# Attention and two MLPs on one core: token blocks of the second MLP widened from 256 to 384

## The chip, the cores and the metric

The kernel runs as one program on one core of a Trainium2 chip. The metric is device time in microseconds (us) of one execution; a kernel's time is the median of its runs. A profiled execution gives besides its own time a span, from the first to the last instruction in the trace.

## What is computed

Everything is float32 outside the kernel. Attention (4 batches, 8 heads, 576 positions, head size 64, with a position bias) gives x with 2304 tokens of 512 values. Two MLPs follow, each fed by the one ahead of it:

```python
def _moe_ref(x, w_in, w_out):          # d_ff = 2048
    h = x @ w_in
    g = h - np.tanh(h)
    return g @ w_out

def _moe2_ref(x, w_gate, w_val, w_out):  # d_ff = 1536
    gate = 1.0 / (1.0 + np.exp(-(x @ w_gate)))
    val = x @ w_val
    return gate * val @ w_out
```

The change concerns the second MLP alone.

## The kernel before

TensorE multiplies in float32r, a form of lower precision, so each operand is split into a high and a low part and every product is made of three matmuls: high by high, low by high and high by low.

The program has three stages: the bias with the attention (the trace's first third), the first MLP, and the second MLP. Both MLPs are one list of steps, `STEPS` (L433 to L435). A step (kind, b, f) treats one block b of `TBS[kind]` tokens and one slice f of the hidden size. In the first MLP (kind 1) a block has 384 tokens and a step two slices of 128 hidden values. In the second (kind 2) a block has 256 tokens before the change, a step one slice of 128, and a block twelve steps (f = 0 to 11): 9 blocks, 108 steps, numbered 48 to 155.

A step of the second MLP passes through these stages, and the main loop of `mlps` puts the stages of several steps into each of its iterations:

- `first` (L589): gate and value projection. For each of the two, 4 parts of the inner size by 3 products, so 24 matmuls, weights stationary, tokens moving: as wide as the block. They write one of two PSUM buffers `up` (L709).
- `second` (L597): sigmoid of the gate on ScalarE (ACT), L611.
- `third` (L613): gate by value on VectorE (DVE), L632; it reads `up` last and so frees it for the `first` two steps on.
- `fourth` (L634): high part by a cast on ACT (L639), low part by a subtraction on GpSimd (POOL, L640).
- `fifth` (L648): output projection. Here the tokens are stationary, 128 at a time, and 512 columns of the weight move: 3 matmuls for each 128 tokens (L670), accumulated over the twelve steps of the block in one PSUM buffer `acc` for each 128 tokens. The pool has four (L720).
- `sixth` (L680): after a block's last step each accumulator is copied to a tile `o`, in turn by ACT (L694) and DVE (L692), and sent to `out` (L698). The pool of `o` has two buffers (L766).

`LAGS` (L771) gives the distances: in iteration n the loop issues `second` of step n-1, `third` of n-2, `fourth` of n-3, then `sixth` of a step that ended a block in the iteration before, `first` of n, and `fifth` of n-4. TensorE therefore does `first`(n), `fifth`(n-4), `first`(n+1), and so on, in that order.

Beside this a stream of weights is prepared: a weight tile is loaded (L484), its magnitude taken on ACT (`scan`, L493), four DVE operations build the float32 value (L508, L509, L510, L506), and ACT and POOL split it (L526, L524). `load` for the next tile is issued when the last DVE operation of one is done. `conv_rate` (L775) gives one or two such tiles for each step. The stream ends in the first block of the second MLP; after that its weights stay in SBUF.

Tokens for the next block are loaded by `x_load` (L564) and split by `x_split` (ACT L570, POOL L571) seven to two steps ahead.

Of the kernel before, what the change touches and what calls it, by code (L numbers as in the profile page):

```python
# [414 lines left out]
KIND = {0: "VV", 2: "V", 4: "VV", 6: "AG", 7: "AG", 8: "AG"}  # L415


TBS = (None, 384, 256)
NF1, NF2 = DF1 // 128, DF2 // 128
FA = 8  # L420
RES = 34
# [10 lines left out]
HALF = FA // NPR  # L432
STEPS = [(1, b, f) for b in range(NT // TBS[1]) for f in range(HALF)]  # L433
STEPS += [(1, b, f) for b in range(NT // TBS[1]) for f in range(HALF, NF1 // NPR)]
STEPS += [(2, b, f) for b in range(NT // TBS[2]) for f in range(NF2)]  # L435
LAST = {(k, f): n for n, (k, b, f) in enumerate(STEPS)}
# [112 lines left out]
def mlps(tc, st, xr, W, xs, x2s, out, consts):  # L549
# [9 lines left out]
    def x_load(blk, kt):  # L559
        kind, b, half = blk  # L560
        TB = TBS[kind]
        m = xr.tile([128, TB], F32, name="xm")
# [4 lines left out]
    def x_split(blk, kt):  # L567
        m = xraw.pop((blk, kt))
        t = xh.tile([128, 2, TBS[blk[0]]], F32R, name="xt")
        A.copy(t[:, 0], m)  # L570
# [9 lines left out]
    def project(w, blk, p):  # L580
        TB = TBS[blk[0]]
        for kt in range(4):
            x = xt[blk, kt]
            for i, (a, c) in enumerate(P3):
                T.matmul(p[:, 0:TB], w[:, a, 128 * kt:128 * kt + 128], x[:, c], start=(kt == 0 and i == 0), stop=(kt == 3 and i == 2))  # L585
# [299 lines left out]
```

## Time and profile before

| what | value |
|---|---|
| median of 3 runs | 1224.86 us (1223.2 to 1227.69) |
| the profiled execution | 1225.91 us |
| its span, first to last instruction | 1224.1 us |
| TensorE matmul busy | 1192.4 us (97%) |
| DVE, ACT, POOL busy | 731.8, 641.1, 570.5 us |
| chain that ended last | PE 88%, DVE 5%, DMA 3%, ACT 2% |
| second MLP in the span | from 745.1 us to the end |

Busy time of TensorE counts a matmul from its start to a modelled end, and neighbours overlap; the cost of a matmul in a stream is read from start to start. A timeline row merges like instructions that follow each other: "x24" has a start, and the time until the last of the 24 ended. "[0.79 <-DVE t L632]" at a row's end is idle time of the engine before it and what ended it.

### The profile page before, as it was taken

How to read it: one execution, taken by the hardware profiler on the slowest of the kernel's cores; microseconds unless marked ns; L12 is line 12 of the kernel's file. 1: busy time of each engine (PE TensorE's matmuls, PEld its weight loads, DVE VectorE, ACT ScalarE, POOL GpSimd, SP SyncE). 2: the span in 40 equal slices, each digit the busy share in tenths (PEclk: the TensorE clock that was granted, in tenths of full speed). 3: DMA queues.
4: the chain of work that ended last, by engine and by line, in shares of the span. 5: the costliest groups of instructions: out<-in, count | busy, mean ns of one | idle time of the engine just before them, and what ended most of it. 6: DMA issues, size and time to landing. Idle time of an engine off the chain costs nothing.

```text
span 1224.1 us, 21207 instructions
## 1 busy us (share of the span) xinstructions
PE 1192.4 (97%) x7856; PEld 1053.9 (86%) x7856; DVE 731.8 (60%) x1292; ACT 641.1 (52%) x1338; POOL 570.5 (47%) x584
## 2 busy tenths in 40 slices
PE   7889999999999999999999999999999999999998
PEld 2257777777679999999999999889999999999997
DVE  6888999999739888988989669851101111011010
ACT  5887888888657667667666564432112121121211
POOL 1049989998635555555645334552122121221211
PEclk9999999999989999999999999999999999999999
DMA  6765747475212333333343313420001000010000
GB/s 188 248 195 149 230 144 215 140 231 151 79 49 87 112 122 107 104 121 103 135 146 130 106 57 109 148 79 13 27 10 35 22 15 26 10 36 18 18 18 18
DMA packets 80631, 120.86 MB, mean 99 GB/s; under 512 B 10256, under 2 KB 55056, under 8 KB 80528
## 3 DMA queue, kind: packets, MB, share of 16 engines
q1 hardware_dynamic: 80528, 119.51, 31.4%
q8 instruction: 62, 1.02, 0.4%
q14 instruction: 41, 0.34, 0.1%
HBM read 89.71 MB, written 29.77 MB: 98 GB/s over the span
## 4 chain that ended last, share of the span: by engine, by line
PE 88%; DVE 5%; DMA 3%; ACT 2%; issue 1%; SPq 0%; POOL 0%; DVEq 0%; ACTq 0%; POOLq 0%
PE up L585 39%; PE acc L662 15%; PE acc L670 11%; PE sc L231 7%; PE pv L323 6%; PE pt L273 6%; PE bt L71 2%; PE pv L320 1%; DMA wraw<-in_wo 1%; DMA bsc<-e 1%; DVE y L66 1%; DVE wu L510 1%; DVE wu L506 1%; DMA wraw<-in_wv 1%; PE pf L277 1%
## 5 line engine op out<-in xcount | busy, mean ns | idle before, releaser
L585 PE MATMUL up<-xt,w 128*128 128x256 f32 (+1 forms) x3744 | 536.3, 299 | 4.7 <-DVE t L632 2.8
L585 PEld LDWEIGHTS up<-xt,w 128*128 128x128 f32 x3744 | 524.7, 190 | 16.3 <-DVE t L632 5.4
L640 POOL TENSOR_TENSOR gl<-t,gh 128x256 fp32r<-128x256 f32 (+1 forms) x204 | 184.7, 914 | 464.7 <-ACT gh L639 296.9
L632 DVE TENSOR_TENSOR t<-up,t 128x256 f32<-128x256 f32 x108 | 45.6, 423 | 319.4 <-ACT t L611 319.4
L611 ACT ACTIVATE t<-up 128x256 f32<-128x256 f32 x108 | 41.5, 384 | 328.0 <-PE up L585 327.8
L662 PE MATMUL acc<-gh,w 128*128 128x384 f32 x768 | 195.8, 335 | 2.9 <-ACT z L604 2.9
L662 PEld LDWEIGHTS acc<-gh,w 128*128 128x128 f32 x768 | 137.9, 188 | 4.8 <-ACT z L604 3.8
L670 PE MATMUL acc<-w,gh 128*128 128x512 f32 x432 | 135.6, 395 | 0.0
L263 POOL TENSOR_SCALAR n<-n,rec 128x576 f32<-128x576 f32 x144 | 117.6, 828 | 26.2 <-ACT n L253 18.4
L662 PE MATMUL acc<-gl,w 128*128 128x384 f32 x384 | 128.3, 334 | 0.0
L253 ACT ACTIVATE n<-n,mn 128x576 f32<-128x576 f32 x144 | 112.6, 782 | 22.9 <-DVE mn L246 21.7
L246 DVE CUSTOM_DVE_ANT_0 n<-sc,bias 128x576 f32<-128x576 f32 x144 | 107.3, 745 | 22.4 <-POOL n L263 13.5
L571 POOL TENSOR_TENSOR xt<-xm,xt 128x384 fp32r<-128x384 f32 (+1 forms) x84 | 75.3, 909 | 71.9 <-ACT xt L570 71.9
L524 POOL TENSOR_TENSOR w<-wu,w 128x512 fp32r<-128x512 f32 x68 | 99.5, 1464 | 12.4 <-ACT w L526 11.1
L639 ACT CAST gh<-t 128x256 fp32r<-128x256 f32 (+1 forms) x204 | 91.4, 453 | 7.5 <-PE acc L662 3.6
L273 PE MATMUL pt<-ident,n 128*128 128x128 f32 x576 | 90.9, 281 | 0.0
L273 PEld LDWEIGHTS pt<-ident,n 128*128 128x128 f32 x576 | 66.8, 142 | 27.6 <-POOL n L263 7.9
L625 ACT ACTIVATE z<-z,c 128x768 f32<-128x768 f32 x48 | 45.2, 942 | 77.7 <-DVE up L624 77.7
L231 PE MATMUL sc<-kh,qs 128*128 128x288 f32 x336 | 81.2, 327 | 3.5 <-DVE mn L246 3.2
L670 PE MATMUL acc<-w,gl 128*128 128x512 f32 x216 | 84.0, 389 | 0.0
L670 PEld LDWEIGHTS acc<-w,gh 128*128 128x128 f32 x432 | 74.5, 190 | 9.8
L626 DVE TENSOR_TENSOR t<-up,t 128x768 f32<-128x768 f32 x48 | 46.0, 958 | 60.9 <-ACT t L604 60.9
(70 smaller groups left out, 1699.3 us busy)
## 6 DMA issues: line engine op xcount, KB each, us to landing
wraw<-in_wo SPq DMA_DIRECT2D x28, 512.0 KB, 3.7
bsc<-e SPq DMA_DIRECT2D x36, 295.5 KB, 3.1
raw<-in_qT SPq DMA_DIRECT2D x64, 144.0 KB, 4.1
raw<-in_kT SPq DMA_DIRECT2D x64, 144.0 KB, 2.9
xm<-xs SPq DMA_DIRECT2D x48, 192.0 KB, 3.6
x2s<-o SPq DMA_DIRECT2D x48, 192.0 KB, 3.9
wraw<-in_wi SPq DMA_DIRECT2D x16, 512.0 KB, 4.4
wraw<-in_wg SPq DMA_DIRECT2D x12, 512.0 KB, 3.7
```

The source lines that it names most:

```text
L231: T.matmul(s[:, hf, x:x + n], w, k_[:, a, y:y + n], start=(i == 0), stop=(i == len(ops) - 1 and x + n == S // 2))
L246: V.tensor_tensor_reduce(n.rearrange("p (a b) -> p a b", a=2), s[:, :, 0:288], bias[t].rearrange("p (a b) -> p a b", a=2), -0.125, 3.0e38, ...
L253: A.activation(n, n, AF.Exp, bias=m, scale=-1.0, accum_out=nsum[u, t // 3][:, t % 3:t % 3 + 1])
L263: G.tensor_scalar(n, n, nrec[u, t // 3][:, t % 3:t % 3 + 1], 1.0, ALU.mult, ALU.mult)
L273: T.transpose(pt[:, i], n[:, o:o + 128], ident)
L524: self.nc.gpsimd.tensor_sub(w[:, 1], u, w[:, 0].bitcast(F32))
L571: G.tensor_sub(t[:, 1], m, t[:, 0].bitcast(F32))
L585: T.matmul(p[:, 0:TB], w[:, a, 128 * kt:128 * kt + 128], x[:, c], start=(kt == 0 and i == 0), stop=(kt == 3 and i == 2))
L639: A.copy(h, x[:, j])
L640: G.tensor_sub(l, x[:, j], h.bitcast(F32))
L662: T.matmul(ac[blk][d][:, 0:TB], w[:, a, 128 * d:128 * d + 128], c, start=(begin and j == 0 and i == 0), stop=(end and j == NPR - 1 and i = ...
L670: T.matmul(ac[blk][d], g[:, c], w[:, a], start=(begin and i == 0), stop=(end and i == 2))
```

## The change

One number: a block of the second MLP has 384 tokens in place of 256.

```diff
@@ -415,7 +415,7 @@
-TBS = (None, 384, 256)
+TBS = (None, 384, 384)
```

What follows from it in the program: 6 blocks for 9, 72 steps for 108 (48 to 119); the 24 matmuls of `first` are 384 wide, 1728 of them for 2592; `fifth` has three accumulators and 9 matmuls for two and 6, 648 of them in both; sigmoid, product, cast and subtraction are 384 wide, 72 of each for 108; `x_load` and `x_split` are 384 wide, 24 for 36; `sixth` has three copies at the end of a block for two, 18 in both, ACT having the first and the third. `conv_rate` and the lags count steps and are the same.

**TensorE, a step within the first block.** The order of its instructions before (`up` is the output of `first`, `acc` of `fifth`, w a weight tile, gh and gl the two parts of the tokens):

```order
L585 MATMUL up<-xt,w_7707 128x256 [waits DVE_49]
L585 MATMUL up<-xt,w_7707 128x256 x11
L585 MATMUL up<-xt,w_7879 128x256 x12
L670 MATMUL acc<-w_7787,gh 128x512 [waits Activation_49]
L670 MATMUL acc<-w_7787,gh 128x512
L670 MATMUL acc<-w_7787,gl 128x512 [waits Pool_49]
L670 MATMUL acc<-w_7787,gh 128x512 x2
L670 MATMUL acc<-w_7787,gl 128x512
```

and now:

```order
L585 MATMUL up<-xt,w_7707 128x384 [waits DVE_49]
L585 MATMUL up<-xt,w_7707 128x384 x11
L585 MATMUL up<-xt,w_7879 128x384 x12
L670 MATMUL acc<-w_7787,gh 128x512 [waits Activation_49]
L670 MATMUL acc<-w_7787,gh 128x512
L670 MATMUL acc<-w_7787,gl 128x512 [waits Pool_49]
L670 MATMUL acc<-w_7787,gh 128x512 x2
L670 MATMUL acc<-w_7787,gl 128x512
L670 MATMUL acc<-w_7787,gh 128x512 x2
L670 MATMUL acc<-w_7787,gl 128x512
```

The same 24 matmuls are wider, and a third accumulator's three matmuls stand behind the two others.

**TensorE, the start of the second block's accumulation**, after the change:

```order
L585 MATMUL up<-xt,w_7159 128x384 [waits DVE_49]
L585 MATMUL up<-xt,w_7159 128x384 x11
L585 MATMUL up<-xt,w_7347 128x384 x12
L670 MATMUL acc<-w_7249,gh 128x512 [waits Activation_49]
L670 MATMUL acc<-w_7249,gh 128x512
L670 MATMUL acc<-w_7249,gl 128x512 [waits Pool_49]
L670 MATMUL acc<-w_7249,gh 128x512 [waits Activation_49]
L670 MATMUL acc<-w_7249,gh 128x512
L670 MATMUL acc<-w_7249,gl 128x512
L670 MATMUL acc<-w_7249,gh 128x512 [waits DVE_49]
L670 MATMUL acc<-w_7249,gh 128x512
L670 MATMUL acc<-w_7249,gl 128x512
```

Before, a new block's two accumulators were both free and only gh and gl were waited for. Now the second and third accumulator wait for ACT's and DVE's copies of the block before; a whole `first` stands between that block's last matmul and these.

**ACT, its last instructions**, before (tiles with their numbers; o and acc are those of `sixth`):

```order
L611 ACTIVATE t_13250<-up_13257 128x256 [waits PE_49]
L639 CAST gh_13289<-t_13175 128x256 [waits DVE_49]
L639 CAST gh_13300<-t_13250 128x256 [waits DVE_49,PE_49]
L639 CAST gh_13311<-t_13250 128x256 [waits DVE_49,PE_49,Pool_49]
L694 COPY o_13327<-acc_13017 128x512 [waits DMAHW5_49,PE_49]
```

and now:

```order
L639 CAST gh_12080<-t_11957 128x384 [waits DVE_49]
L639 CAST gh_12094<-t_12038 128x384 [waits DVE_49,PE_49]
L639 CAST gh_12108<-t_12038 128x384 [waits DVE_49,PE_49,Pool_49]
L694 COPY o_12130<-acc_11783 128x512 [waits DMAHW2_49,DMAHW0_49,PE_49]
L694 COPY o_12136<-acc_11785 128x512 [waits DMAHW2_49,PE_49,Activation_49]
```

ACT has a second copy, of the third accumulator, and it waits for a DMA: with two buffers, its tile o is the one that the first copy filled, and that must have been sent.

## Rows read from the trace of the kernel before

**Rows 1.** The page, parts 1 and 2: busy time of engines; granted clock by slice.
```profile
PE 1192.4 (97%) x7856; PEld 1053.9 (86%) x7856; DVE 731.8 (60%) x1292; ACT 641.1 (52%) x1338; POOL 570.5 (47%) x584
...
PEclk9999999999989999999999999999999999999999
```

**Rows 2.** Stages: busy us by engine, clock, DMA share, GB/s; in the second MLP.
```profile
1000.00:1100.00 100.00, 100.00 (x704) 93.81 (x703) 11.39 (x26) 19.89 (x58) 22.45 (x31) 1.00 0.07 22
```

**Rows 3.** Timeline of PE (start, us, engine, line, operation, tiles), last steps to the end.
```profile
1206.24 3.04 PE L585 MATMUL up<-xt,w 128*128 128x256 f32 x24
1209.11 0.63 PE L670 MATMUL acc<-w,gh 128*128 128x512 f32 x2
...
1210.50 3.04 PE L585 MATMUL up<-xt,w 128*128 128x256 f32 x24
...
1219.29 0.39 PE L670 MATMUL acc<-w,gl 128*128 128x512 f32 x1
...
1219.97 0.39 PE L670 MATMUL acc<-w,gl 128*128 128x512 f32 x1
```

**Rows 4.** Timeline of PE, a step of the first MLP, 384 wide.
```profile
728.49 4.32 PE L585 MATMUL up<-xt,w 128*128 128x384 f32 x24
732.65 0.51 PE L662 MATMUL acc<-gh,w 128*128 128x384 f32 x2
...
736.81 4.32 PE L585 MATMUL up<-xt,w 128*128 128x384 f32 x24
```

**Rows 5.** Timeline of PE, first block of the second MLP: some starts of `first`.
```profile
745.13 3.03 PE L585 MATMUL up<-xt,w 128*128 128x256 f32 x24
...
754.24 3.11 PE L585 MATMUL up<-xt,w 128*128 128x256 f32 x24 [1.91 <-DVE t L630]
...
772.17 3.14 PE L585 MATMUL up<-xt,w 128*128 128x256 f32 x24 [0.31 <-DVE t L632]
...
777.48 3.14 PE L585 MATMUL up<-xt,w 128*128 128x256 f32 x24 [0.79 <-DVE t L632]
...
814.32 3.04 PE L585 MATMUL up<-xt,w 128*128 128x256 f32 x24
```

**Rows 6.** Timelines of DVE, SP and ACT in the same stretch.
```profile
753.11 0.99 DVE L630 COPY_PREDICATED t<-z,up 128x768 f32<-128x768 int32 x1
...
771.84 0.38 SPq L484 DMA_DIRECT2D wraw<-in_wv  x1
...
775.96 0.66 ACT L493 ACTIVATE wu<-wraw 128x512 f32<-128x512 f32 x1 [2.95 <-DMA wraw<-in_wv]
776.53 0.37 ACT L611 ACTIVATE t<-up 128x256 f32<-128x256 f32 x1
...
777.00 0.42 DVE L632 TENSOR_TENSOR t<-up,t 128x256 f32<-128x256 f32 x1 [1.00 <-ACT t L611]
```

**Rows 7.** Timelines of ACT, SP, DVE at the end; landing time of `out` (L698).
```profile
1219.72 0.59 ACT L694 COPY o<-acc 128x512 f32<-128x512 f32 x1 [3.17 <-PE acc L670]
...
1220.33 1.12 SPq L698 DMA_DIRECT2D out<-o  x2
...
1220.40 0.69 DVE L692 COPY o<-acc 128x512 f32<-128x512 f32 x1 [5.99 <-PE acc L670]
...
DMA to landing us min/median/max: 2.0/2.0/2.5
```

**Rows 8.** Groups by line and shape: count, busy us, mean ns, idle before.
```profile
L632 DVE TENSOR_TENSOR t<-up,t 128x256 f32<-128x256 f32 x108 | 45.6, 423 | 319.4 <-ACT t L611 319.4
L688 DVE TENSOR_TENSOR o<-acc,o 128x384 f32<-128x384 f32 x24 | 11.6, 548 | 0.0
...
L639 ACT CAST gh<-t 128x384 fp32r<-128x384 f32 x96 | 48.4, 515 | 6.0 <-PE acc L662 3.6 <-DVE t L630 2.2
L640 POOL TENSOR_TENSOR gl<-t,gh 128x384 fp32r<-128x384 f32 x96 | 102.7, 1088 | 141.8 <-issue 75.3 <-PE acc L662 36.1 <-ACT gh L639 19.4
```

**Rows 9.** Timelines of DVE and PE, a block's end in the first MLP.
```profile
596.33 1.94 DVE L688 TENSOR_TENSOR o<-acc,o 128x384 f32<-128x384 f32 x4
...
597.02 0.58 PE L662 MATMUL acc<-gh,w 128*128 128x384 f32 x2 [0.98 <-ACT z L604]
```

**Rows 10.** The issues of `x_load` (L564): landing time.
```profile
DMA to landing us min/median/max: 1.9/3.1/5.0
```

## The prediction

> **What bounds the kernel now.** I read the page first. TensorE is busy for 97% of the span and its granted clock stays at 9 tenths or more of full speed in every slice [rows 1], the 2.4 GHz level. In the second MLP nothing else comes near: in a stretch of 100 us PE is busy for all of it at a clock of 1.00, while ACT has 19.89 us, POOL 22.45 and DVE 11.39 [rows 2]. So the price of a step there is what TensorE's own stream costs, and I read that from start to start in the timeline, not from busy time.
>
> A steady step: `first` starts at 1206.24 us, its `fifth` at 1209.11, the next `first` at 1210.50 [rows 3]. That is 2.87 us for 24 matmuls of 256 columns (119.6 ns each), 1.39 us for 6 of 512, and 4.26 us together. From the `first` at 814.32 [rows 5] to the one at 1210.50 lie 93 steps and 396.18 us, 4.26 each: no waits at all in that stretch. The first MLP has the same operation at the new width: 728.49 to 732.65 is 4.16 us for 24 matmuls of 384 columns, 173.3 ns each, and the 24 behind them take 4.16 us too [rows 4].
>
> Ahead of 814.32 it is not steady. From the first `first` (745.13) to 814.32 lie 69.19 us [rows 5]. They hold 14 `first` (40.18 us), 10 `fifth` of the second MLP (13.90) and two of the first MLP, 24 matmuls of 384 each (8.32): 62.40 us of work. The other **6.79 us are waits**, all for DVE. The largest is at 754.24, where TensorE is ready at 745.13 + 2.87 + 4.16 = 752.16 and waits 2.08 us for the last operation of the first MLP's `third`, which DVE ends at 754.10 [rows 5, 6]. The other 4.7 us come from the weight stream. Rows 6 show one such chain: the load issued at 771.84 lands, ACT scans the weight at 775.96 and only then reaches the sigmoid (776.53), the product follows at 777.00, and `first` starts at 777.48 after a step of 5.31 us [rows 5], the longest of that stretch. TensorE waits there because this chain is longer than its step.
>
> The end: the last matmul starts at 1219.97 and is done at 1220.36 [rows 3]; ACT has copied the first accumulator from 1219.72, DVE copies the second until 1221.09 [rows 7], and the span ends 3.01 us after that, at 1224.1.
>
> **The change, part by part.** *The matmuls.* A new step is 4.16 us for 24 matmuls of 384 [rows 4] and 9 of 512. Three matmuls of one accumulator take 0.68 us (1219.29 to 1219.97 in rows 3), so `fifth` goes from 1.39 to 2.07 and the step to 6.23 us. 108 x 4.26 = 460.08 becomes 72 x 6.23 = 448.56: **11.52 us less**. The columns streamed are the same; what goes is a fixed part of each matmul. By rows 3 and 4 it is 119.6 - 256/2.4 = 12.9 ns at 256 columns, 173.3 - 160 = 13.3 at 384, and 13.3 at 512, and 864 matmuls fewer at 13.3 ns are again 11.5 us.
>
> The Trainium skill speaks against a gain of that size: "TensorE: Matmul & The Clock Gate", section "Wait — 56ns, not 53.3ns?", gives a full-clock matmul its columns over 2.4 GHz and a fixed 2.5 ns. By that the 864 matmuls would give back an estimated 2.2 us. The trace disagrees, with 12.9 to 13.3 ns at three widths, and I take the trace.
>
> *The waits of the first block.* The weight stream is counted in steps, and the steps get longer. The chain of 5.31 us grows by the wider sigmoid and product, about 0.13 us each (423 ns at 256 columns, 548 for a DVE operation of 384 that reads PSUM too [rows 8]), to 5.57 us; the new step has 6.23. So TensorE no longer comes too early. The wait at 754.24 shrinks: DVE ends L630 at the same time, and TensorE is ready at 745.13 + 4.16 + 4.16 = 753.45, so 0.79 us remain. 6.79 becomes 0.79: **6.0 us less**. The bounds are 6.79 (nothing waits) and 0 (every wait stays as long as it is); I take 6.0, since the longest chain shown fits the new step.
>
> *The accumulators.* The second and third accumulator of a new block were the first and second of the last one. At a block's end E (its last matmul done) ACT's copy of the first is done at E - 0.7 and DVE's of the second at about E, with the durations of rows 7 and groups of 0.68 us. TensorE wants them after a `first` of 4.16 us and one or two groups of 0.68. Nothing, with 4 us in hand.
>
> *The third copy.* It needs the tile o that the first copy filled, so ACT waits until that is sent, 2.0 to 2.5 us [rows 7]. Inside the kernel that costs nothing: ACT is done at about E + 2.0, and behind it on ACT stands the sigmoid of the `first` that ends at E + 4.16. On SP's queue the third `out` waits too, and behind it the loads of the next block's tokens, which are wanted seven steps later. At the kernel's end nothing covers it. The first accumulator is done two groups ahead of E, its copy runs from E - 1.32 to E - 0.73, its transfer lands by E + 1.3, the third copy of 0.59 us ends at about E + 2.0, and with the 3.01 us from there the span ends at E + 5.0, where it was E + 3.74: **1.3 us more**. The bounds are -0.1 (if the copy did not wait: E + 0.63 + 3.01) and +1.7 (landing in 2.5).
>
> *The rest.* Cast and subtraction are 515 and 1088 ns at 384 columns [rows 8]; with sigmoid and product that is under 3 us between `first`(n) and a `fifth` four steps later, covered by three steps of 6.23, and at the end, where no `first` is left, by four `fifth` of 2.07. The token loads are larger and fewer, with landings of 5.0 us at most [rows 10] against steps of 6.23. If that cover were gone, one load would cost its landing time once per block.
>
> **The sum.** -11.52 - 6.0 + 1.3 = -16.2 us on the profiled execution's 1225.91: 1209.7. That execution lies 1.05 us above the median of the runs, 1224.86; against the median it is **1208.7 us**, 1.3% faster.
>
> **The rivals.** *The first block keeps its waits* (the weight stream's chain stretches with the steps): 6.0 us more, 1214.7. For it speaks that loads, scans and sigmoids stand in one line on ACT; against it that the longest chain fits the new step.
>
> *The accumulators run short.* In the first MLP a block takes all four, and TensorE waits 0.98 us at a block's end until DVE has begun to empty them at 596.33 [rows 9]. Five inner block ends at that price are 4.9 us: 1213.6. Against it: one of four is free here, a `first` lies between, and DVE is nearly idle.
>
> *The fixed part does not shrink*, that is, a matmul costs by its columns alone in this stage: 11.52 us are not won, 1220.2. Rows 4 speak against it, with the same line at 384 columns. By the page's 2.5 ns, weighed above, it would be an estimated 1218.
>
> *Slower: ACT stuck behind the output transfers.* At each inner block end ACT's queue stands until the first copy's transfer has landed. TensorE first misses something when the sigmoid behind it is so late that `up` is not free for the second `first` after, 4.16 + 2.07 + 6.23 = 12.46 us after E, less 1.2 for sigmoid and product. With the copies that needs a landing time of about 11.4 us. At 14 us the five ends would lose 2.6 each and the kernel's end 12 more: about 1234. The longest landings shown are 2.5 for `out` and 5.0 for the tokens [rows 7, 10].
>
> *No effect*: the block is not really wider, 1224.9. The order shows the wide matmuls.
>
> **How the numbers follow.** Forecast 0.84, waits stay 0.06, accumulators 0.04, fixed part 0.02, slower 0.02, no effect 0.02. A measurement of this kernel tells about 0.5% from no change, 6 us. Faster by more than that: the first three, 0.94; within: 0.04; slower: 0.02. The range takes the bounds of the tail (1207.3 to 1209.1), the scatter of the runs of before (1.7 us below and 2.8 above the median), and upward most of the way to the first two rivals: 1205.5 to 1213.5.
>
> **What would show it.** In the profile after: L585 only at 384 columns in the second MLP, 1728 times; starts of `first` 6.23 us apart from the second block on, without a gap at block ends; 0.8 us of wait at the second `first` and next to none behind it; ACT's third copy standing about 2 us behind the first with `out` as its releaser, and the span ending 5 us after the last matmul. Wrong would be: steps above 6.3 us, idle time of PE released by a copy of `acc` or by the product at L632 after the first block, or a clock below 1.00 there.

## The result and the profile after

| | median | runs |
|---|---|---|
| before | 1226.04 us | 4, from 1223.2 to 1227.69 |
| changed | 1212.60 us | 4, from 1211.55 to 1214.16 |

The ratio is 0.9894 with a 95% interval of 0.9870 to 0.9918: 13.4 us less by the medians, where 16.2 were forecast, and clear of the 0.5% that the prediction takes as the least change that can be told here. The profiled execution took 1213.29 us with a span of 1211.5.

The page of the changed kernel, its first lines, answers to [rows 1]:

```profile
PE 1181.9 (98%) x6992; PEld 1044.7 (86%) x6992; DVE 725.4 (60%) x1253; ACT 632.0 (52%) x1257; POOL 559.8 (46%) x536
...
PEclk9999999999989999999999999999999999999999
...
L585 PE MATMUL up<-xt,w 128*128 128x384 f32 x2880 | 520.6, 335 | 0.6 <-DVE t L630 0.6
```

On the page of before the last of these lines was

```profile
L585 PE MATMUL up<-xt,w 128*128 128x256 f32 (+1 forms) x3744 | 536.3, 299 | 4.7 <-DVE t L632 2.8
```

TensorE issues 864 matmuls fewer (7856 to 6992), and all 2880 of L585 are 384 wide now. TensorE is still the bound, and its granted clock is 1.00 through the second MLP, as before. Its idle time ahead of L585 fell from 4.7 to 0.6 us, and DVE's product at L632 releases none of it any more. What TensorE waited for from 720 us on (us in total, times, the longest), before and then after:

```profile
PE up L585 <- DVE t L632: 2.8, 4, 0.9
PE up L585 <- DVE t L630: 1.9, 1, 1.9
```

```profile
PE up L585 <- DVE t L630: 0.6, 1, 0.6
```

These lists count idle time from the modelled end of a matmul, so they hold 4.7 of the 6.79 us that the starts gave before.

The timeline of TensorE in the changed kernel, first block of the second MLP, answers to [rows 5]:

```profile
746.03 4.32 PE L585 MATMUL up<-xt,w 128*128 128x384 f32 x24
755.09 4.40 PE L585 MATMUL up<-xt,w 128*128 128x384 f32 x24 [0.58 <-DVE t L630]
763.49 12.64 PE L585 MATMUL up<-xt,w 128*128 128x384 f32 x72
778.05 4.35 PE L585 MATMUL up<-xt,w 128*128 128x384 f32 x24
784.32 4.35 PE L585 MATMUL up<-xt,w 128*128 128x384 f32 x24
790.58 4.35 PE L585 MATMUL up<-xt,w 128*128 128x384 f32 x24
```

The wait for L630 has shrunk: TensorE is ready at 746.03 + 8.32 = 754.35 and starts at 755.09, so 0.74 us where 2.08 stood. From 778.05 on the steps are equal, 6.27 us each; the four waits for L632 are gone. The weight stream's chain is still there. ACT and DVE in the same stretch of the changed kernel, the same kind of scan as in [rows 6]:

```profile
777.39 0.68 ACT L493 ACTIVATE wu<-wraw 128x512 f32<-128x512 f32 x1 [2.88 <-DMA wraw<-in_wv]
777.96 0.49 ACT L611 ACTIVATE t<-up 128x384 f32<-128x384 f32 x1
...
778.55 0.56 DVE L632 TENSOR_TENSOR t<-up,t 128x384 f32<-128x384 f32 x1
```

ACT stands 2.88 us for the load, where it stood 2.95 before, and the product is done at 779.11. The `first` that wants this `up` stands two steps on and starts at 784.32, 5.2 us later, so nothing waits.

A steady step and the end, TensorE, then ACT, SP and DVE; they answer to [rows 3] and [rows 7]:

```profile
1183.30 0.63 PE L670 MATMUL acc<-w,gh 128*128 128x512 f32 x2
...
1185.38 4.35 PE L585 MATMUL up<-xt,w 128*128 128x384 f32 x24
1189.57 0.63 PE L670 MATMUL acc<-w,gh 128*128 128x512 f32 x2
...
1191.65 4.35 PE L585 MATMUL up<-xt,w 128*128 128x384 f32 x24
...
1205.85 0.39 PE L670 MATMUL acc<-w,gl 128*128 128x512 f32 x1
```

```profile
1204.92 0.59 ACT L694 COPY o<-acc 128x512 f32<-128x512 f32 x1 [4.43 <-PE acc L670]
1207.65 0.59 ACT L694 COPY o<-acc 128x512 f32<-128x512 f32 x1 [2.15 <-DMA out<-o]
...
1205.53 3.07 SPq L698 DMA_DIRECT2D out<-o  x3
...
1205.60 0.69 DVE L692 COPY o<-acc 128x512 f32<-128x512 f32 x1 [8.48 <-PE acc L670]
```

`first` takes 4.19 us (1185.38 to 1189.57), `fifth` 2.08 (to 1191.65): 6.27, against 6.23 in the sum. The last matmul is done at 1206.24 and the span ends at 1211.5, 5.26 us behind it; before that was 3.74. The row with "2.15 <-DMA out<-o" is the third copy standing for the first one's transfer.

So the two profiled executions, 12.62 us apart, differ in three places. The second MLP's first matmul starts 0.90 us later (746.03 for 745.13), which is within the 2.9 us by which this start scatters among the profiles of the experiments below. From there to the last matmul it is 460.21 us for 475.23: 15.02 less. After the last matmul it is 1.52 more.

### The profile page after: what moved, and what is told of

Its sections match the earlier page's. It is cut to its first block, busy times and chain, and to the rows that moved or that the text cites. A ratio compares the mean times of both kernels' runs of the same rounds, so it can differ in the third digit from the quotient of the medians.

```text
span 1211.5 us, 19227 instructions
## 1 busy us (share of the span) xinstructions
PE 1181.9 (98%) x6992; PEld 1044.7 (86%) x6992; DVE 725.4 (60%) x1253; ACT 632.0 (52%) x1257; POOL 559.8 (46%) x536
## 4 chain that ended last, share of the span: by engine, by line
PE 92%; DMA 2%; DVE 2%; ACT 2%; issue 1%; POOL 0%; SPq 0%; ACTq 0%; DVEq 0%; POOLq 0%
PE up L585 41%; PE acc L662 16%; PE acc L670 12%; PE sc L231 7%; PE pv L323 6%; PE pt L273 6%; PE bt L71 3%; PE pv L320 1%; DMA bsc<-e 1%; PE pf L277 1%; DMA bias<-bsc 1%; DVE y L66 0%; ACT y L64 0%; ACT z L604 0%; PE pf L281 0%
## 5 line engine op out<-in xcount | busy, mean ns | idle before, releaser
L585 PE MATMUL up<-xt,w 128*128 128x384 f32 x2880 | 520.6, 335 | 0.6 <-DVE t L630 0.6
L585 PEld LDWEIGHTS up<-xt,w 128*128 128x128 f32 x2880 | 503.7, 188 | 7.4 <-PE acc L662 0.9
L640 POOL TENSOR_TENSOR gl<-t,gh 128x384 fp32r<-128x384 f32 x168 | 176.1, 1060 | 470.6 <-ACT gh L639 338.4
L632 DVE TENSOR_TENSOR t<-up,t 128x384 f32<-128x384 f32 x72 | 40.1, 557 | 309.2 <-ACT t L611 309.2
L611 ACT ACTIVATE t<-up 128x384 f32<-128x384 f32 x72 | 35.4, 492 | 331.9 <-PE up L585 331.9
L571 POOL TENSOR_TENSOR xt<-xm,xt 128x384 fp32r<-128x384 f32 x72 | 73.8, 1040 | 65.9 <-ACT xt L570 65.7
L670 PEld LDWEIGHTS acc<-w,gh 128*128 128x128 f32 x432 | 80.1, 188 | 13.5
L639 ACT CAST gh<-t 128x384 fp32r<-128x384 f32 x168 | 84.8, 511 | 8.4 <-PE acc L662 3.6
```

What stands on the lines that cost most here:

```text
L571: G.tensor_sub(t[:, 1], m, t[:, 0].bitcast(F32))
L639: A.copy(h, x[:, j])
L640: G.tensor_sub(l, x[:, j], h.bitcast(F32))
L670: T.matmul(ac[blk][d], g[:, c], w[:, a], start=(begin and i == 0), stop=(end and i == 2))
```

## The experiments

All edits are made on the changed kernel. The first four and the blocks of 128 tokens were run once each; a single time scatters by a few us, since the second MLP starts at 743.46 to 746.36 us in the profiles of this section. What is compared is therefore the time from the start of the second MLP to the last matmul (460.21 us in the changed kernel), and from there to the span's end (5.26).

### Three buffers for o

```diff
-            ob = st.enter_context(tc.tile_pool(name="p3o", bufs=2))
+            ob = st.enter_context(tc.tile_pool(name="p3o", bufs=3))
```

> The changed kernel with three buffers for o in place of two, so that the third copy of a block waits for no transfer. My theory: the wait costs only at the kernel's end, about 1.5 us there (span end 5.3 us after the last matmul becomes 3.8), and nothing at the five inner block ends: steps of `first` stay 6.27 us apart. Rival (ACT standing behind the transfer delays the steps): the starts of `first` move closer after block ends too, and the gain is several us.

1211.95 us. ACT at the end of this kernel:

```profile
1204.67 0.59 ACT L694 COPY o<-acc 128x512 f32<-128x512 f32 x1 [4.43 <-PE acc L670]
1206.03 0.59 ACT L694 COPY o<-acc 128x512 f32<-128x512 f32 x1 [0.77 <-PE acc L670]
```

The third copy now waits only for its accumulator. From the last matmul (1205.60 + 0.39) to the span's end (1210.2) it is 4.21 us: 1.05 less, not 1.5. From the second MLP's start to the last matmul it is 460.16 us, as before. The wait is real and costs only at the end. Of its 2.15 us, 0.77 stay, because the accumulator is not done before; the copy ends 0.63 us after the last matmul instead of 2.00, which is 1.37 earlier. The span wins 1.05 of that: the three transfers now follow each other more closely, and the last takes 2.5 us to land, where it took 2.2.

### One buffer for o

```diff
-            ob = st.enter_context(tc.tile_pool(name="p3o", bufs=2))
+            ob = st.enter_context(tc.tile_pool(name="p3o", bufs=1))
```

> The changed kernel with one buffer for o, so that every copy of a block waits for the transfer ahead of it: the suspected wait is doubled. My theory: about 3 us more, all after the last matmul (span end some 8 us after it); at inner block ends TensorE still waits for nothing, since the second accumulator is free about 2 us after the block's end and wanted after 4.9. Rival (output buffers and accumulators bind at inner ends): gaps on TensorE at the five inner block ends, 1 us or more each, so 8 us or more in all.

1214.78 us. What ACT waits for in the second MLP's steady part of this kernel, and its last copy:

```profile
ACT o L694 <- DMA out<-o: 25.6, 5, 5.4
...
1209.06 0.58 ACT L694 COPY o<-acc 128x512 f32<-128x512 f32 x1 [5.02 <-DMA out<-o]
```

At the five inner block ends ACT now stands for 25.6 us in all, 5.4 the longest; with two buffers it was 10.9. TensorE has no wait at all in that stretch, and start to last matmul is 460.06 us. The end grows to 8.22 us, 3.0 more. So a wait of ACT more than twice as long still hides at every inner end. The forecast's rival for the slower side is bounded from this side: up to 5.4 us of standing do nothing; its point of decision near 11 us was not reached by any run.

### No spare accumulator

```diff
-            ac[blk] = [acc.tile([128, 512], F32, name="acc") for _ in range(4 if kind == 1 else TB // 128)]
+            ac[blk] = [acc.tile([128, 512], F32, name="acc") for _ in range(4)][:4 if kind == 1 else TB // 128]
```

> The changed kernel, with a block taking four accumulators and using three, so that the next block begins in the bank that the last block's first accumulator had: no spare one. My theory: no change (within the scatter of 2 us, steps of 6.27 us at block ends too), because a whole `first` of 4.19 us covers the copy. Rival (the fourth bank is what keeps TensorE from waiting): gaps at the five inner block ends, about 1 us each as in the first MLP, 5 us in all.

1210.81 us; 460.21 us from start to last matmul, the same to the hundredth; no wait of TensorE after the first block. The fourth bank does nothing here. The reading that fits is that the `first` of 4.19 us between two blocks covers the copies; no run took that `first` away. The first MLP's order has such a `first` too. There DVE was at other work until 596.33, and TensorE went on just after DVE's first addition had ended at 596.87 [rows 9]; the row names an ACT operation, which ended at the same time, but what TensorE's queue stood for there is DVE's count.

### The order in pairs

```diff
         for m in due(n, 2):
-            fifth(m)
+            if STEPS[m][0] == 1:
+                fifth(m)
+            elif n % 2:
+                fifth(m - 1)
+                fifth(m)
```

> The changed kernel with TensorE's order in the second MLP in pairs: `first`, `first`, `fifth`, `fifth` in place of `first`, `fifth`. Theory A (the 0.04 us that a step has over 4.16 + 2.07 belongs to each turn between the 384-wide and the 512-wide matmuls): a pair of steps takes 12.47 us in place of 12.53, about 2 us less in all. Theory B (it belongs to the matmuls of this stage themselves): 12.53 as before, no gain. Slower if `up` comes free too late for the second `first` of a pair: then idle time of PE released by DVE L632.

1211.24 us. TensorE in steady pairs of this kernel:

```profile
784.39 8.51 PE L585 MATMUL up<-xt,w 128*128 128x384 f32 x48
796.86 8.51 PE L585 MATMUL up<-xt,w 128*128 128x384 f32 x48
809.32 8.51 PE L585 MATMUL up<-xt,w 128*128 128x384 f32 x48
```

12.47 us a pair against 12.53. From start to last matmul it is 457.88 us, 2.3 less, with no wait for L632. That is theory A's figure, and it speaks for its cause, the turns, but the 0.04 us of a step are not the whole surcharge: with half of them gone a pair would take 12.50. In stretches without turns the parts of a step are 4.16 us and three times 0.68, 6.20 together. The plain order takes 0.07 us more than that in each step and the pairs 0.03: half the turns, half the surcharge. The 1.39 of the forecast's `fifth`, read behind a turn, already held the part that the 0.04 leave out.

The starts of single matmuls in the changed kernel's trace show the same. The first six of `first` take 1.07 us and its last six 1.04; from the seventh on they are 173 ns apart. The nine of `fifth` take 2.08 us, and nine at the program's end, where `fifth` follows `fifth`, 2.04. What in TensorE makes a turn cost that was not tried.

### Wide blocks first, or last

Blocks of the second MLP with sizes of their own (start and size from a list, in place of `TBS[kind] * b` and `TBS[kind]` everywhere):

```diff
+CUT = [(0, 384), (384, 384)] + [(768 + 256 * b, 256) for b in range(6)]
...
+def span(kind, b):
+    return (384 * b, 384) if kind == 1 else CUT[b]
...
-STEPS += [(2, b, f) for b in range(NT // TBS[2]) for f in range(NF2)]
+STEPS += [(2, b, f) for b in range(len(CUT)) for f in range(NF2)]
```

> The second MLP's first two blocks have 384 tokens, the six after them 256. My theory: the waits of the first block go (6.0 us), 24 steps of 6.27 replace 36 of 4.26 (2.95 us), the end has two copies as before (0): 9.0 us less than the kernel before, about 1217.0. Rival (all of the gain is the number of matmuls): 3 us less.

1216.57 us against 1225.95, ratio 0.9928 (0.9909 to 0.9947): 9.4 less, 9.0 expected. The rival's 3 us are far outside.

For the other kernel the list is `[(256 * b, 256) for b in range(6)] + [(1536, 384), (1920, 384)]`.

> The second MLP's first six blocks have 256 tokens, the last two 384. My theory: the waits of the first block stay (0), the matmuls give the same 2.95 us, the third copy at the end costs 1.5: 1.4 us less than the kernel before, about 1224.6. Rival (the waits of the first block cost the end nothing, since work behind them makes it up): as much gain as with the wide blocks first.

1224.36 us, ratio 0.9992 (0.9980 to 1.0003): 1.6 less, 1.4 expected; the interval alone would also allow no change. What TensorE waited for in the second MLP, with the wide blocks first and then with them last (here `first` is at L592, `third`'s operations at L637 and L639):

```profile
PE up L592 <- DVE t L637: 0.9, 1, 0.9
```

```profile
PE up L592 <- DVE t L639: 2.9, 4, 1.2
PE up L592 <- DVE t L637: 1.9, 1, 1.9
```

The same number of matmuls was taken away in both; only where the wide blocks stand differs, and with it 7.8 us by the medians. The waits of the weight stream go only if the block in which it runs is the wide one. By their own traces, wide first and then wide last, it is 466.43 us from the second MLP's start to the last matmul against 472.09, 5.7 less, and from there to the span's end 4.25 against 5.51, 1.3 less, since only the second kernel has a third copy at its end. The remaining 0.8 us of the medians no trace assigns.

### Blocks of 128 tokens

```diff
-TBS = (None, 384, 384)
+TBS = (None, 384, 128)
```

> Blocks of 128 tokens in the second MLP: the fixed part of a matmul at a third width. Theory A (128 columns at 2.4 GHz and a fixed 13.3 ns): `first` takes 24 x 66.7 = 1.60 us and a steady step about 2.30 us; 216 steps make the kernel some 36 us slower plus the waits of the first block, which get longer. Theory B (the weight load, rows of 188 to 192 ns each with two under way, sets the distance): at least 94 ns each, `first` 2.26 us or more, a step about 2.95, over 170 us slower.

2119.57 us, 894 more than before: outside both theories, and by a way neither had. TensorE's clock on the page of this kernel, five of its stages (the columns are those of [rows 2]), and rows of its timeline:

```profile
PEclk9999999999999995555555555555555555555555
```

```profile
740.00:760.00 20.00, 17.98 (x104) 17.69 (x103) 18.15 (x23) 10.73 (x19) 9.11 (x8) 0.84 0.45 143
...
785.00:790.00 5.00, 5.00 (x42) 4.56 (x41) 3.22 (x5) 1.13 (x3) 3.00 (x3) 1.00 0.58 156
790.00:795.00 5.00, 3.95 (x31) 3.45 (x30) 4.39 (x9) 2.62 (x9) 2.59 (x5) 0.97 0.34 99
795.00:800.00 5.00, 5.00 (x22) 4.71 (x22) 2.86 (x6) 1.75 (x5) 3.67 (x5) 0.50 0.59 194
...
1500.00:2000.00 500.00, 500.00 (x2111) 477.35 (x2111) 22.74 (x78) 45.06 (x187) 45.58 (x102) 0.50 0.03 8
```

```profile
753.61 5.24 PE L585 MATMUL up<-xt,w 128*128 128x128 f32 x24 [2.02 <-DVE t L630]
...
763.78 8.15 PE L585 MATMUL up<-xt,w 128*128 128x128 f32 x72
771.77 0.67 PE L670 MATMUL acc<-w,gh 128*128 128x512 f32 x2
...
784.77 2.90 PE L585 MATMUL up<-xt,w 128*128 128x128 f32 x24 [1.18 <-DVE t L632]
...
793.09 3.94 PE L585 MATMUL up<-xt,w 128*128 128x128 f32 x24 [1.05 <-DVE t L632]
...
1502.22 5.21 PE L585 MATMUL up<-xt,w 128*128 128x128 f32 x24
1507.12 0.55 PEld L670 LDWEIGHTS acc<-w,gh 128*128 128x128 f32 x2
1507.23 1.16 PE L670 MATMUL acc<-w,gh 128*128 128x512 f32 x2
...
1508.62 5.21 PE L585 MATMUL up<-xt,w 128*128 128x128 f32 x24
```

At the full clock 72 matmuls of 128 columns take 7.99 us (763.78 to 771.77), 111 ns each. The fixed part of 13 ns gives 66.7, so at this width something else sets the distance; theory B's lower end of 94 is nearer. The Trainium skill, "TensorE: Matmul & The Clock Gate", section "LDWEIGHTS (loading the stationary operand)", puts a load of 128 columns at its columns over 1.2 GHz, an estimated 107 ns. The measured 111 is near that, but no run here varied the loads alone, and the profile's rows give a load 192 ns, the next begun 111 ns behind it. At half the clock, below, the same matmuls are 209 ns apart, which 107 does not give. What sets the distance at this width stays open.

The granted clock fell twice, to 0.50, the 1.2 GHz level. The first time was just behind the wait of 2.02 us for L630; the clock was 0.50 from 754 to 760 us and 1.00 again from 762, while matmuls of 384 columns of the first MLP ran. In the kernel before, a wait of 2.08 us at that place had left it at 1.00. The second time was in a stretch with waits for DVE of 1.18 and 1.05 us between bursts of narrow matmuls. From then on it stayed at 0.50 to the last matmul, though TensorE is busy there without a gap. A step for 128 tokens then takes 6.40 us (1502.22 to 1508.62); its 24 narrow matmuls alone are some 5.0 (to 1507.23), where they had been 2.7. This is one run, and no other tried what made the clock fall.

### Pairs and three buffers

Both edits together.

> Both small edits on the changed kernel: order in pairs and three buffers for o. My theory: 1.5 us less at the end and, if the turns carry the 0.04 us of a step, 2 us less before it: 1209 us, against 1212.6 of the changed kernel; 1211 if they do not.

1208.88 us (5 runs, 1205.8 to 1210.42) against 1225.95, ratio 0.9857 (0.9837 to 0.9878). From start to last matmul 457.93 us, from there to the end 4.22: both gains stand side by side. It is the fastest of all the kernels run, 3.7 us below the changed one by the medians of different sessions; by the traces of the two it should be 3.3.

## Why the prediction was right, and where its size was off

- **The bound and the side.** Right: TensorE's own stream, at the full clock, sets the time of the second MLP before and after, and the change shortens that stream.
- **The matmuls: 11.52 us forecast, 9.0 measured.** This is the term that was mis-sized. From the second MLP's start to the last matmul 15.02 us went, 6.05 of them waits, so 8.97 are the steps. The failing step of the working is "so `fifth` goes from 1.39 to 2.07 and the step to 6.23 us". Its parts came from stretches without turns: the 4.16 us of `first` from the first MLP, where all widths are 384 [rows 4], and the third group's 0.68 us from the program's last matmuls [rows 3]. In the alternating stream they are 4.19 and 0.69. The old step of 4.26 had been read where it runs, with its turns. 0.036 us for each of 72 steps are the missing 2.6 us; the order in pairs and the single starts showed that turns carry them. The second way to the sum, 864 matmuls at 13.3 ns, agreed with the first because it leaves the turns out as well.
- **The fixed part of a matmul.** It goes with the number of matmuls, as taken, and the 384-wide ones settle at 173 ns in this stage too. Away from turns, starts are 120.0, 173.3 and 226.7 ns apart at 256, 384 and 512 columns: 13.3 ns on top of the columns at 2.4 GHz at each width, the forecast's 12.9 being read behind a turn. The Trainium skill's 2.5 ns ("TensorE: Matmul & The Clock Gate", "Wait — 56ns, not 53.3ns?") would have left an estimated 2.2 us for this term; the traces hold 9.0. But 13 ns on top of the columns is a law for 256 to 512 columns only: 128 columns take 111 ns.
- **The waits of the first block: 6.0 forecast, 6.05 measured** (6.79 to 0.74; 0.79 was expected to stay). 1.34 of them are the shorter wait for L630, the other 4.71 those that the forecast gave to the weight stream. That these belong to the place and not to the whole was shown by the wide blocks first and last. That it is the stream that makes them is read from the traces, where the chain stands ahead of the wait before and has 5.2 us in hand after; no run took the stream away.
- **The accumulators and the inner block ends: nothing, and nothing was found**, with four banks, with no spare one, and with ACT standing some 5 us at each.
- **The end: 1.3 forecast, 1.52 measured**, of which a third buffer gives back 1.05. The third copy ended 2.00 us after the last matmul, as forecast; from there to the span's end it was 3.26 us, where 3.01 had been taken.
- **The rivals.** None came in. "The fixed part does not shrink" and "the accumulators run short" fell by the steps of 6.27 us without a gap; "the first block keeps its waits" by the list of waits.
- **The time.** 1208.7 was forecast and 1212.6 measured, inside the range. 2.8 us of the distance are the gain that fell short. The other 1.2 come from the yardstick: against the first three runs of before, whose median the forecast used, one more run moved that median from 1224.86 to 1226.04.

## What to carry to other kernels

Where one engine's stream is the bound, cost a wider tile by the instructions it saves times their fixed part, and read both old and new step in a stream that alternates as the real one does; prices from uniform stretches miss what the turns cost. Then look at what runs beside the stream: here 4.71 of the 15.02 us came from a preparation that is counted in steps, and a longer step gave it time. A copy that waits for its own output buffer is free as long as a longer stage covers it, and shows at the program's end, where nothing does.

## What the runs showed of the hardware

- A turn between 384-wide and 512-wide matmuls costs: two steps take 12.53 us in plain order and 12.47 with half the turns, on a stream that has no other gap. The six matmuls behind a turn to 384 columns take 1.07 us, six later ones 1.04.
- Matmuls of 128 columns in this stream take 111 ns at the full clock, against 120 for 256 columns, so halving the width saves almost nothing.
- With the blocks at 128 tokens TensorE's clock fell to 1.2 GHz and stayed there for more than 1300 us while its busy share was 100% (one run). In the kernels with 256 and 384 columns the second MLP kept the full clock throughout. A busy share of 100% says nothing of the clock; read the granted clock beside it.
